# One kernel, several loads reordered: q in one transfer, words behind k and v, the last tile's stores issued by GpSimd

## The chip, the cores and the metric

The kernel runs on one core of a Trainium2 chip. The core has five engines that run their own instruction streams and meet through semaphores: TensorE (PE in the profile; PEld is its loading of weights), VectorE (DVE), ScalarE (ACT), GpSimd (POOL) and SyncE (SP). Here SyncE computes nothing and issues transfers. The transfers of all issuing engines run on the core's 16 DMA engines. The metric is the device time of one execution in microseconds; lower is better. The time before the change is the median of 3 runs, 886.57 us (884.79 to 888.91).

## The reference

```python
def _attn_ref(q, k, v, g_norm):                      # q, k, v: 8 batches, 8 heads, 576 tokens, 64
    kv = np.einsum('bhsd,bhse->bhde', k, v)
    out = np.einsum('bhsd,bhde->bhse', q, kv)
    rms = np.sqrt(np.mean(out * out, axis=-1, keepdims=True) + 1e-06)
    return (out / rms * g_norm).astype(np.float32)

def _moe_ref(x, w_in, w_out):                        # x: 4608 x 512; w_in: 512 x 2048; w_out: 2048 x 512
    h = x @ w_in
    sp = np.where(h > 20.0, h, np.log1p(np.exp(np.minimum(h, 20.0))))
    g = h * np.tanh(sp)
    return (g @ w_out).astype(np.float32)
```

The attention result is laid out as one row of 512 for each of the 4608 tokens and is x of the second function. g_norm is float32 of length 64. The two weight matrices are float64: the kernel sees them as pairs of 32-bit words and joins them to float32 itself.

## The kernel before, in words

Both matrix products of the second function are done by a recursive scheme with 7 block products in place of 8 (Strassen–Winograd). The names A11, S1, S2, A12, S4, S3, A22 are its left operands, and B11, T1 and so on its right ones. To keep fp32 accuracy, each operand is split into a high part (a cast on ScalarE, line 121) and a low part (a subtraction on VectorE, line 122), and each block product is three matmuls per 128 rows.

**Part 1** makes x, and g = mish(x @ w_in), in 9 tiles of 512 tokens. A tile has 4 groups of 7 slots, and so 28 slots in all (`NS`); a group makes g for two of the eight column blocks of each half. A slot is one block product on TensorE (12 matmuls, line 527). `slot(t)` first issues what evicts finished banks (`then`), then the product, then what stands in the plan for that slot (`at`). The order of all engines' work is this order of the program, written out by hand: an instruction waits for everything that stands before it on its engine or queue, and nothing is reordered.

The weights go through `weight_forms` (lines 128 to 178): LOAD (transfers of words by SyncE, line 137), SCALE (ScalarE, line 142), JOIN (three VectorE steps, lines 147 to 149), DIFF (157 to 159), BLOCKS and SUMS (splits, lines 121 and 122). For w_in they are numbered 0 to 7. The words of weights 2 and 5 share the room `wf6`, those of 3 and 6 the room `wf7`, those of 0, 4 and 7 the room `w64`; a load into a room waits until JOIN has read what was there. Weights 0, 1 and 2 are made before slot 0; weights j from 3 to 7 have SCALE and JOIN at slot 3(j−3)+1.

Before slot 0, q of tile 0 comes in four transfers of 128 tokens (`rows_load`, line 295). A partition holds one token of each, and its 64 numbers of a head are one piece of 256 bytes. TensorE turns it with 16 transposes (line 325), the results are copied out (`turned`), and `kv_first_product` (line 234) makes the first batch's product of k and v; `kv_keep` (line 269) copies it out of PSUM, `project` (line 360) multiplies q by it; squares, sums, logarithm and exponential follow (lines 373, 391, 408, 409) and `normalize` (line 430). Tile 1 is loaded and turned in the same way, into one bank pair `x2` for each of its two units, at slots 1 and 8. From tile 2 on (`T32 = 2`) the tiles take another path, which the change leaves alone.

k and v of batch 1 come in four pairs (`k_load`, lines 213 and 214). There are two sets of staging tiles, so the third pair waits for the product of the first (`k_product`, line 252). The last two pairs are issued at slots 1 and 2, their products stand at slots 2 and 3. The loads of weights 6 and 7 stand at slots 1 and 4; in slot 1 the load stands ahead of the third pair of k and v on SyncE's queue.

Each group's results leave by three stores to the DRAM tile `gd` (`put_in`, lines 546, 551, 554), out of the tiles `ula`, `ulb` and `ur`, two buffers each: a buffer is written again two groups later. SyncE issues these stores for tiles 0 to 7, ScalarE those of tile 8.

**Part 2** multiplies g by w_out in 18 groups of 256 tokens. Its preparation runs during tile 8, whose first slot is t8: `g_load(0)` and `g_load(1)` (line 731, 2048 KB each) bring g of the first two groups at slots t8+7 and t8+8. `wo_load` (line 726, 1792 KB each) brings the eight made weights of w_out into the places of w_in's, which come free group by group: two at each of t8+10, t8+17 and t8+24, two at the end. At t8+18, `g_pair` makes the first seven forms for group 0, all in that slot. Group 0 runs as one product over all eight weights (line 863), the others as 7 block products each (line 772). `o_store` (line 793 for tiles 0 and 1, line 804 for the others) writes the output.

Of the kernel before, what the change touches and what calls it, by code (L numbers as in the profile page):

```python
# [27 lines left out]
def linear_attention_rms_mish_ffn(  # L28
# [260 lines left out]
    def rows_load(j, c):  # L289
        for b, s0, cols in segments(j):  # L290
            t0, t1 = max(cols.start, c * P), min(cols.stop, (c + 1) * P)
            if t0 < t1:
                src = q[b, 0:1, s0 + t0 - cols.start:s0 + t0 - cols.start + 1, :]
                src = bass.AP(src.tensor, src.offset, [[D, t1 - t0], [S * D, H], [1, D]])
                nc.sync.dma_start(rows[j][t0 - c * P:t1 - c * P, c, :].rearrange("p (h d) -> p h d", d=D), src)
# [4 lines left out]
    def unit_steps(j, u):  # L300
# [14 lines left out]
        def transpose():  # L315
            if j < T32:
                if j == 0 and u == 1:
                    ps = [bank_new("a").rearrange("p m t -> p (m t)") for _ in range(2)]
                else:
                    x2 = ps_t.tile([P, 2, T], F32, name="x2")  # L320
                    ps = [x2[:, a] for a in range(2)]
                for a in range(2):
                    h = 4 * u + 2 * a
                    for c in range(TR):
                        nc.tensor.transpose(ps[a][:, c * P:(c + 1) * P], rows[j][:, c, h * D:(h + 2) * D], ident)
# [24 lines left out]
        def project():  # L350
# [120 lines left out]
    def at(t, f):  # L471
        plan.setdefault(t, []).append(f)
# [118 lines left out]
    rows[0], turned_q = t[:, 0:2].rearrange("p a (c n) -> p (a c) n", c=TR // 2), t[:, 2].rearrange("p (a t) -> p a t", a=2)  # L591
    for c in range(TR):
        rows_load(0, c)
# [40 lines left out]
    rows[1] = att.tile([P, TR, H * D], F32, name="qs")  # L634
    for c in range(TR):
        rows_load(1, c)
# [7 lines left out]
    weights(2, DIFF)  # L644
    weights(5, LOAD)
# [137 lines left out]
    def o_store(st):  # L783

        i, half = divmod(st["s"], T // G)
        if i < T32:
            for r in range(G // P):
                c = half * G // P + r
                for b, s0, cols in segments(i):
                    t0, t1 = max(cols.start, c * P), min(cols.stop, (c + 1) * P)  # L790
                    if t0 < t1:
                        row = b * S + s0 + t0 - cols.start
                        nc.sync.dma_start(out[row:row + t1 - t0, :], st["o"][t0 - c * P:t1 - c * P, r, :])
            return
# [28 lines left out]
    at(t8 + 8, lambda: g_load(1))  # L823
    at(t8 + 18, lambda: g_pair(gs[0], 0, pair_rooms(0)))
# [128 lines left out]
```

## Time and profile before

| | |
|---|---|
| median of 3 runs | 886.57 us (884.79, 886.57, 888.91) |
| the profiled execution | 885.97 us, span 884.2 us, mean granted clock 0.987 |
| TensorE, matmuls | 828.1 us busy (94%) |
| TensorE, weight loads | 795.7 us (90%) |
| VectorE | 608.7 us (69%) |
| ScalarE | 464.6 us (53%) |
| GpSimd | 4.8 us (1%), 23 instructions, all within the first 6 us |
| DMA | 175.5 MB, mean 199 GB/s |

Times in the rows of the profile are microseconds from the span's start. A row of the timeline gives start, duration, engine, line, operation, what is written and read, and in brackets how long the engine had stood idle before it and what ended that. SPq and ACTq are the queues on which SyncE and ScalarE issue transfers; their rows give issue times, not the time that the data moves. A row of waits gives total, number and longest wait. The chain of waits is followed back from the last instruction and told in order of time. A busy TensorE isn't TensorE at its peak, because matmuls are pipelined.

### The profile page before, as it was taken

The page shows a single profiled execution, that of the slowest core. Times are in us where ns is not written, and L with a number is a line of the kernel's source. Part 1 is how long each engine was busy: PE and PEld are TensorE (multiplying, and loading weights), DVE is VectorE, ACT ScalarE, POOL GpSimd, SP SyncE. Part 2 cuts the span into 40 slices and gives each one's busy share as a digit, 9 for nine tenths or more (in the row PEclk, how much of TensorE's full clock was granted, in tenths as well). Part 3 has the DMA queues.
Part 4 walks back from the last instruction along what each step waited for, and adds up shares of the span by engine and source line. Part 5 has one row for each costly group of instructions (what it writes and reads, how often), then busy time and mean ns, then how long its engine had stood idle before and what let it go on. Part 6 is the DMA issues. An engine that isn't in the chain of part 4 may idle for free.

```text
span 884.2 us, 17156 instructions
## 1 busy us (share of the span) xinstructions
PE 828.1 (94%) x7036; PEld 795.7 (90%) x7036; DVE 608.7 (69%) x804; ACT 464.6 (53%) x703; POOL 4.8 (1%) x23
## 2 busy tenths in 40 slices
PE   4658998998999999999999899999999999999997
PEld 3447898998999999999999789999999999999997
DVE  5869675886777676787764368867777677776772
ACT  3647666556675765666664444344444434434431
POOL 2000000000000000000000000000000000000000
PEclk9969999999999999999999999999999999999999
DMA  9936787987978696767477993344434443334421
GB/s 294 247 114 197 200 274 246 278 263 226 296 219 278 218 304 199 220 204 227 151 227 249 425 416 125 122 150 152 148 121 133 130 120 120 119 120 141 153 65 48
DMA packets 161038, 175.52 MB, mean 199 GB/s; under 512 B 24704, under 2 KB 142464, under 8 KB 159936
## 3 DMA queue, kind: packets, MB, share of 16 engines
q1 hardware_dynamic: 158208, 170.23, 61.8%
q10 hardware_dynamic: 2752, 4.20, 1.3%
q8 instruction: 55, 0.90, 0.4%
q14 instruction: 23, 0.19, 0.1%
HBM read 112.39 MB, written 62.00 MB: 197 GB/s over the span
## 4 chain that ended last, share of the span: by engine, by line
PE 63%; DMA 11%; DVE 10%; ACT 9%; issue 4%; SPq 2%; ACTq 0%; DVEq 0%
PE a L772 22%; PE bc L772 16%; PE a L527 13%; PE bc L527 7%; DMA gd<-ula 5%; PE s L252 2%; DMA vm<-in_v_dram 2%; DVE ur L548 1%; DMA wod<-wst 1%; ACT L412 1%; ACT gf L121 1%; DMA rd<-fl 1%; DVE gf L122 1%; DVE fa L122 1%; ACT L118 1%
## 5 line engine op out<-in xcount | busy, mean ns | idle before, releaser
L772 PE MATMUL a<-wf,gf 128*128 128x256 f32 x1632 | 201.8, 283 | 0.5 <-DVE ur L812 0.5
L772 PEld LDWEIGHTS a<-wf,gf 128*128 128x128 f32 x1632 | 198.4, 192 | 0.7 <-DVE ur L812 0.7
L122 DVE TENSOR_TENSOR gf<-g,gf 128x1024 fp32r<-128x1024 f32 (+1 forms) x123 | 132.9, 1087 | 90.7 <-ACT gf L121 90.7
L527 PE MATMUL a<-gf,wf 128*128 128x256 f32 x1296 | 173.0, 287 | 11.5 <-DVE gf L430 4.5
L527 PEld LDWEIGHTS a<-gf,wf 128*128 128x128 f32 x1296 | 162.9, 193 | 18.1 <-ACT ur L504 6.6
L527 PE MATMUL bc<-gf,wf 128*128 128x256 f32 x1296 | 170.3, 285 | 3.5 <-ACT ur L495 2.4
L527 PEld LDWEIGHTS bc<-gf,wf 128*128 128x128 f32 x1296 | 161.4, 191 | 5.1 <-ACT ur L495 2.6
L121 ACT CAST gf<-g 128x1024 fp32r<-128x1024 f32 (+1 forms) x123 | 114.6, 939 | 93.3 <-DVE g L752 65.1
L772 PE MATMUL bc<-wf,gf 128*128 128x256 f32 x1224 | 152.7, 283 | 1.0 <-DVE gf L122 1.0
L772 PEld LDWEIGHTS bc<-wf,gf 128*128 128x128 f32 x1224 | 149.4, 192 | 1.4 <-ACT gf L121 0.7
L527 PE MATMUL a<-a,wf 128*128 128x256 f32 x432 | 59.8, 289 | 2.5 <-DVE ur L548 2.5
L527 PEld LDWEIGHTS a<-a,wf 128*128 128x128 f32 x432 | 55.8, 195 | 5.6 <-DVE ur L548 3.1
L118 ACT ACTIVATE ur<-ur 128x1024 f32<-128x1024 f32 x36 | 38.1, 1059 | 37.1 <-DVE ur L548 37.1
L122 DVE TENSOR_TENSOR fa<-fl,fh 128x1024 fp32r<-128x1024 f32 x28 | 34.3, 1224 | 22.1 <-ACT fh L121 21.2
L504 ACT COPY ur<-a 128x512 f32<-128x512 f32 (+1 forms) x53 | 27.3, 516 | 37.6 <-PE a L772 24.6
L122 DVE TENSOR_TENSOR gf<-gf 128x512 fp32r<-128x512 f32 x45 | 30.4, 689 | 24.0 <-ACT gf L121 24.0
L121 ACT CAST gf<-a 128x1024 fp32r<-128x1024 f32 x17 | 17.9, 1052 | 53.5 <-DVE a L749 50.9
L121 ACT CAST gf<-gf 128x512 fp32r<-128x512 f32 x45 | 27.1, 618 | 31.4 <-DVE gf L451 19.1
L495 ACT COPY ur<-bc 128x512 f32<-128x512 f32 (+1 forms) x53 | 27.4, 517 | 29.9 <-PE bc L772 23.0
L548 DVE TENSOR_TENSOR ula<-bc,ula 128x512 f32<-128x512 f32 x36 | 24.8, 688 | 25.4 <-PE bc L527 25.3
L118 ACT ACTIVATE ula<-ula 128x512 f32<-128x512 f32 x36 | 22.8, 633 | 22.1 <-DVE ula L548 22.1
L252 PE MATMUL s<-vm,km 128*64 128x64 f32 x448 | 20.1, 235 | 14.1 <-DMA vm<-in_v_dram 14.1
(137 smaller groups left out, 858.1 us busy)
## 6 DMA issues: line engine op xcount, KB each, us to landing
g<-gd SPq DMA_DIRECT2D x18, 2048.0 KB, 8.9
gd<-ur SPq DMA_DIRECT2D x32, 512.0 KB, 4.0
wod<-wst SPq DMA_DIRECT2D x16, 896.0 KB, 5.6
wf<-wod SPq DMA_DIRECT2D x8, 1792.0 KB, 16.2
gd<-ula SPq DMA_DIRECT2D x32, 256.0 KB, 5.1
gd<-ulb SPq DMA_DIRECT2D x32, 256.0 KB, 4.3
w<-in_moe_w_out_dram SPq DMA_DIRECT2D x32, 256.0 KB, 4.6
km<-in_k_dram SPq DMA_DIRECT2D x28, 256.0 KB, 4.8
```

Source lines behind the costliest of these rows:

```text
L118: nc.scalar.activation(o, i, AF.Mish)
L121: nc.scalar.copy(hi, src)
L122: nc.vector.tensor_sub(lo, src, hi.bitcast(F32))
L252: nc.tensor.matmul(kvps[o * D:(o + 1) * D, b % 2, h0 // 2 + i, :], kt, vt, start=(c == 0), stop=(c == CM))
L412: nc.scalar.preload_act_table_set("natural_log_exp_and_others")
L495: then(t + 2, lambda: nc.scalar.copy(dst(st, "22"), st["c"]))
L504: then(t + 4, lambda: nc.scalar.copy(dst(st, "12"), st["a"]))
L527: nc.tensor.matmul(bank[:, jj], w[:, right, a, kc, :], xf[:, b, kc, :], start=first and jj == kc == s == 0, stop=(kc == 1 and s == 2), ski ...
L548: nc.vector.tensor_add(o, bank, o)
L772: nc.tensor.matmul(bank, gf[:, a, c, :], wo[c][:, right, b, :], start=first and c == s == 0, stop=(c == NF2 - 1 and s == 2), skip_group_ch ...
```

## The change

- q of tiles 0 and 1 comes in one transfer for each segment (one for tile 0, two for tile 1). A partition now holds four neighbouring tokens, so that a piece is 1024 bytes. Columns of these two tiles therefore stand in another order; `project` picks a segment's columns out by a view, and `o_store` writes rows back in their order, two rows in one piece.
- A turn of 128 columns by a transpose becomes two matmuls against the identity, one for each head, with 64 columns of q as the stationary operand and the identity as the moving one.
- The copies `turned` of unit 1 go ahead of the SUMS of weights 0; SCALE and JOIN of weights 1 go behind the first `kv_keep`.
- The loads of g_norm are issued by GpSimd instead of SyncE, ahead of its other work.
- The load of weights 4 moves from before slot 0's preparation to its end, ahead of that of weights 5. The loads of weights 6 and 7 move from slots 1 and 4 to slots 3 and 6.
- The stores of tile 8 are issued by GpSimd instead of ScalarE.
- `g_load(1)` moves from slot t8+8 to t8+26; the first forms of part 2's group 0 are made one per slot, at t8+17 to t8+23.

```diff
+    def spots(cols):
+
+        return slice(cols.start // TR, cols.stop // TR)
+
+    def rows_load(j):
         for b, s0, cols in segments(j):
-            t0, t1 = max(cols.start, c * P), min(cols.stop, (c + 1) * P)
-            if t0 < t1:
-                src = q[b, 0:1, s0 + t0 - cols.start:s0 + t0 - cols.start + 1, :]
-                src = bass.AP(src.tensor, src.offset, [[D, t1 - t0], [S * D, H], [1, D]])
-                nc.sync.dma_start(rows[j][t0 - c * P:t1 - c * P, c, :].rearrange("p (h d) -> p h d", d=D), src)
+            p = spots(cols)
+            src = q[b, 0:1, s0:s0 + 1, :]
+            src = bass.AP(src.tensor, src.offset, [[TR * D, p.stop - p.start], [S * D, H], [1, TR * D]])
+            nc.sync.dma_start(rows[j][p], src)
...
-                    h = 4 * u + 2 * a
                     for c in range(TR):
-                        nc.tensor.transpose(ps[a][:, c * P:(c + 1) * P], rows[j][:, c, h * D:(h + 2) * D], ident)
+                        for o in range(2):
+                            src = rows[j][:, 4 * u + 2 * a + o, c * D:(c + 1) * D]
+                            nc.tensor.matmul(ps[a][o * D:(o + 1) * D, c * P:(c + 1) * P], src, ident, start=True, stop=True)
...
-                        nc.tensor.matmul(ps[:, c], kvf[b][:, hp, :], st["q"][:, a, c], start=True, stop=True)
+                        o, r = (t.rearrange("p (c n) -> p c n", n=P)[:, :, spots(c)] for t in (ps, st["q"][:, a]))
+                        nc.tensor.matmul(o, kvf[b][:, hp, :], r, start=True, stop=True)
...
-        eng = nc.sync if i < NT - 1 else nc.scalar
+        eng = nc.sync if i < NT - 1 else nc.gpsimd
...
-    for c in range(TR):
-        rows_load(0, c)
+    rows_load(0)
...
-        nc.sync.dma_start(gcol[r, :], g_norm.rearrange("(p o) -> p o", o=1))
+        nc.gpsimd.dma_start(gcol[r, :], g_norm.rearrange("(p o) -> p o", o=1))
     weights(2, LOAD)
-    weights(4, LOAD)
     weights(3, LOAD)
...
     do(0, 0, "turned")
+    do(0, 1, "turned")
     weights(0, SUMS)
-    do(0, 1, "turned")
-    weights(1, SCALE, JOIN)
     kv_first_product(first)
     kv_keep(0, first)
+    weights(1, SCALE, JOIN)
     do(0, 0, "project", "square")
...
     weights(2, DIFF)
+    weights(4, LOAD)
     weights(5, LOAD)
...
-            at(t, lambda j=j: weights((6, 7)[j - 3], LOAD))
+            at(t + 2, lambda j=j: weights((6, 7)[j - 3], LOAD))
...
+            for b, s0, cols in segments(i):
+                p = spots(cols)
+                row = b * S + s0 + half * G // P
+                dst = out[row:row + 1, :]
+                dst = bass.AP(dst.tensor, dst.offset, [[TR * DM, p.stop - p.start], [DM, G // P], [1, DM]])
+                nc.sync.dma_start(dst, st["o"][p])
...
-    at(t8 + 8, lambda: g_load(1))
-    at(t8 + 18, lambda: g_pair(gs[0], 0, pair_rooms(0)))
+    at(t8 + 26, lambda: g_load(1))
+    first_rooms = []
+    for n, f in enumerate(MADE):
+        def first_form(f=f):
+            if f == MADE[0]:
+                first_rooms.extend(pair_rooms(0))
+            gs[0]["f"][f, 0] = g_form(gs[0], f, slice(0, 2), first_rooms[f // 4][:, f % 4])
+        at(t8 + 17 + n, first_form)
```

More of the change, by code (lines that the diff above doesn't have):

```diff
@@ L287, in segments @@
         return segs
-    def rows_load(j, c):
+    def spots(cols):
+        return slice(cols.start // TR, cols.stop // TR)
+    def rows_load(j):
         for b, s0, cols in segments(j):
-            t0, t1 = max(cols.start, c * P), min(cols.stop, (c + 1) * P)
-            if t0 < t1:
-                src = q[b, 0:1, s0 + t0 - cols.start:s0 + t0 - cols.start + 1, :]
-                src = bass.AP(src.tensor, src.offset, [[D, t1 - t0], [S * D, H], [1, D]])
-                nc.sync.dma_start(rows[j][t0 - c * P:t1 - c * P, c, :].rearrange("p (h d) -> p h d", d=D), src)
+            p = spots(cols)
+            src = q[b, 0:1, s0:s0 + 1, :]
+            src = bass.AP(src.tensor, src.offset, [[TR * D, p.stop - p.start], [S * D, H], [1, TR * D]])
+            nc.sync.dma_start(rows[j][p], src)
     rows = {}
@@ L590, in linear_attention_rms_mish_ffn @@
     t = wfp.tile([P, 3, 2 * T], F32, name="wf2")
-    rows[0], turned_q = t[:, 0:2].rearrange("p a (c n) -> p (a c) n", c=TR // 2), t[:, 2].rearrange("p (a t) -> p a t", a=2)
-    for c in range(TR):
-        rows_load(0, c)
+    rows[0], turned_q = t[:, 0:2].rearrange("p a (h n) -> p (a h) n", h=H // 2), t[:, 2].rearrange("p (a t) -> p a t", a=2)
+    rows_load(0)
     kv0 += [wfp.tile([P, NKC, 9 * D], F32, name=f"wf{n}") for n in (3, 4)]
@@ L633, in linear_attention_rms_mish_ffn @@
     k_load(1, 1)
-    rows[1] = att.tile([P, TR, H * D], F32, name="qs")
-    for c in range(TR):
-        rows_load(1, c)
+    rows[1] = att.tile([P, H, TR * D], F32, name="qs")
+    rows_load(1)
     do(0, 1, "square", "sums")
@@ L786, in o_store @@
         if i < T32:
[L787 to L793, printed above, removed]
+            for b, s0, cols in segments(i):
[4 more added lines that the diff above has]
+                nc.sync.dma_start(dst, st["o"][p])
             return
```

## The prediction

> **What bounds the kernel now.** First view: TensorE's waits over the whole span (us in total, times, longest); the row on top:
>
> ```profile
> PE s L252 <- DMA vm<-in_v_dram: 14.1, 3, 12.9
> ```
>
> TensorE is otherwise nearly always busy, so its gaps are what an edit of order can win. Of the 14.1 us that it waits for v, 12.9 are one wait, for batch 1. The second view, the timeline around it:
>
> ```profile
> 35.19 12.57 SPq L137 DMA_DIRECT2D wf<-in_moe_w_in_dram  x4
> ...
> 45.55 1.23 DVE L149 SCALAR_TENSOR_TENSOR fl<-wf,fl 128x1024 uint32<-128x1024 uint32 x1
> ...
> 47.86 0.45 SPq L213 DMA_DIRECT2D km<-in_k_dram  x1
> ...
> 51.73 1.22 DVE L122 TENSOR_TENSOR wf<-wd,wf 128x1024 fp32r<-128x1024 f32 x1
> ...
> 54.62 1.12 PE L252 MATMUL s<-vm,km 128*64 128x64 f32 x16 [12.88 <-DMA vm<-in_v_dram]
> ...
> 59.05 0.58 ACT L504 COPY ur<-a 128x512 f32<-128x512 f32 x1 [7.70 <-PE a L527]
> ...
> 60.69 0.69 DVE L147 TENSOR_SCALAR fl<-fl 128x1024 uint32<-128x1024 uint32 x1 [7.74 <-ACT fl L142]
> ...
> 71.75 1.22 PE L325 MATMUL x<-ident,qs 128*128 128x128 f32 x8 [2.54 <-ACT gf L378]
> ```
>
> SyncE holds four word transfers from 35.19 on: weights 5 and weights 6. Weights 6 go into the room that weights 3 are read from, and the last reader is the join at L149, done at 46.78. The k and v loads of slots 1 and 2 stand behind them in SyncE's order, so they leave at 47.86 and v is used at 54.62. But VectorE had work of its own until 52.95 (the L122 at 51.73), and idled only 7.7 us before 60.69. That is the part of the 12.9 us that nothing else covers.
>
> Third, the last tile, where the loads for part 2 run:
>
> ```profile
> 472.34 2.29 SPq L731 DMA_DIRECT2D g<-gd  x2
> ...
> 478.31 34.25 SPq L726 DMA_DIRECT2D wf<-wod  x8
> ...
> 497.39 1.69 PE L527 MATMUL bc<-gf,wf 128*128 128x256 f32 x12 [1.11 <-DVE ula L548]
> ...
> 501.11 1.70 PE L527 MATMUL a<-gf,wf 128*128 128x256 f32 x12 [0.59 <-ACT ula L490]
> ...
> 505.96 0.58 ACT L495 COPY ur<-bc 128x512 f32<-128x512 f32 x1 [4.91 <-DMA gd<-ur]
> ...
> 506.60 1.70 PE L527 MATMUL bc<-gf,wf 128*128 128x256 f32 x12 [2.36 <-ACT ur L495]
> ...
> 510.52 1.70 PE L527 MATMUL a<-a,wf 128*128 128x256 f32 x12 [0.78 <-DVE ur L548]
> ...
> 524.57 0.41 ACT L121 CAST gf<-g 128x256 fp32r<-128x256 f32 x1 [2.94 <-issue]
> ...
> 534.03 3.04 PE L772 MATMUL a<-wf,gf 128*128 128x256 f32 x24
> ...
> 480.00:532.00 52.00, 45.84 (x372) 44.62 (x371) 24.05 (x55) 21.21 (x45) 0.00 (x0) 1.00 1.01 407
> ```
>
> The last row is a view by stretches (PE, PEld, DVE, ACT, POOL busy, clock, DMA share, GB/s): the DMA engines are full. A store of the last tile takes 14 to 23 us, its buffer comes free late, and ScalarE, which also issues these stores, stands still.
>
> **The change part by part.** The profiled execution took 885.97 us (span 884.2 and 1.8 around it), 0.6 below the median of 886.57; I sum against it.
>
> *k and v ahead of the words.* Weights 6 and 7 move two slots back. The two k and v pairs then leave when their staging buffers come free, after the products at 36.47 and 39.77, about 38 and 41. Ahead of them in the queues lie weights 4 (moved here) and 5, 2.1 MB, some 6 us at the 350 to 380 GB/s that the start shows. In the chain of waits v lands 5.4 us after its issue:
>
> ```profile
> 49.06 5.43 DMA vm<-in_v_dram
> ```
>
> There it had the words of weights 6 ahead of it; with another 3 us for what is left of weights 4 and 5, it lands near 44 to 48. VectorE needs the next product (L527, slot 3) out of the way by about 51, so VectorE's order decides: gain **7.7 us**. Bounds: 12.9 if VectorE's order gave way too, 4 if the loads land near 51. Next late is ScalarE's L378 before L325, as now. Weights 4, 6 and 7 are wanted at slots 4, 10 and 13, over 10 us after they can land.
>
> *First q by one transfer.* Each descriptor grows from 256 B to 1 KB. The rates by 1.5 us slices of the first 60 us:
>
> ```profile
> GB/s 0 126 384 320 220 218 239 378 384 358 358 389 361 325 363 348 352 351 346 317 289 185 183 231 218 280 359 93 0 0 5 12 232 382 331 284 238 7 0 0
> ...
> 10.99 1.33 PE L325 MATMUL x<-ident,wf 128*128 128x128 f32 x5 [0.60 <-DMA wf<-in_q_dram]
> ...
> 12.11 1.91 PE L325 MATMUL a<-ident,wf 128*128 128x128 f32 x8
> ...
> 14.35 2.39 PE L234 MATMUL s<-wf,wf 64*64 64x64 f32 x72 [0.32 <-DMA wf<-in_v_dram]
> ...
> 36.47 1.12 PE L252 MATMUL s<-vm,km 128*64 128x64 f32 x16
> ...
> 39.77 0.69 PE L252 MATMUL s<-vm,km 128*64 128x64 f32 x16
> ...
> 40.65 1.09 PE L325 MATMUL x<-ident,qs 128*128 128x128 f32 x8
> ```
>
> q ran at about 220 GB/s, beside 384 before and after. The words and q are 2.1 MB: reached near 9.8 us now, and at 384 from 3 us on near 8.0. The last rows were used 1.2 us behind, so all of q is there at 9.2 instead of 11.0. But the first quarter was used at 7.59; now nothing turns before 9.2. v, and with it the first k·v product, could start near 12.5 instead of 14.35.
>
> *The turns by matmul.* One transpose (16 for a tile) becomes two fp32 matmuls of 64 columns against the identity, and each fp32 matmul is two instructions here (36 at L234 show as 72). So 32 instructions replace 8 for each of the two units. The trace has none of this shape. Nearest: L252, with the same 128*64 weights but 64 moving columns, 43 ns each (0.69/16), 70 ns after a pause. With 128 moving columns I take twice that: 86 and 140 ns. Below stands half of a present turn (two column halves side by side): 0.136/2 = 68 ns, early 0.239/2 = 120. Above: a whole one, 136 and 239. The early price lasts 3.4 us here (10.99 to about 14.4). From 9.2, 64 instructions then take 3.4 us for the first 24 and 40·0.086 = 3.4: done at 16.0, against 14.02 now; bounds 15.0 and 19.4. So TensorE's turns, not v, hold the first product: **+2.0** (+1.0 to +5.4).
>
> *Words of weights 1 after the first kv_keep.* The order on ScalarE now:
>
> ```profile
> 17.32 1.12 ACT L142 ACTIVATE fl<-wf 128x1024 f32<-128x1024 f32 x1 [3.01 <-DMA wf<-in_moe_w_in_dram]
> ...
> 18.34 0.51 ACT L269 COPY kvf<-s 64x128 f32<-64x128 f32 x2
> ...
> 23.75 1.05 ACT L121 CAST wf<-wd 128x1024 fp32r<-128x1024 f32 x1
> ...
> 24.82 1.27 ACT L408 ACTIVATE fa<-bc,eps 128x512 f32<-128x512 f32 x2
> ```
>
> The product ends at 16.74, yet L269 waits for the scale to 18.34. Counted from the end of the turns (14.02), the logarithms of L408 start at +10.8. New order: product to +2.7, keep to +3.25, scale to +4.4, join 3.2 (to +7.6), differences 1.55 (L157 to L159, +9.2), cast 1.05, L408 at +10.25. Gain **0.55**, so the start is 1.45 later in sum (+0.45 to +4.85). From there VectorE has hardly a gap to 52.95, and the delay carries through.
>
> *Second turns of tile 1.* Those of unit 0 stand at 40.65, before the v wait, and cost nothing while v lands after about 43 (1.7 us if that cover is gone). Those of unit 1 are the 1.22 us at 71.75, behind which the chain of waits runs on TensorE alone: 32·0.086 = 2.75, **+1.5** (+0.95 to +3.1).
>
> *Last tile.* Moving the second g (2.1 MB, 5.1 us at 0.41 MB/us) behind six of the eight word loads takes it out of the line that the stores of the second group stand in. That stores share that line is read from their landing (the first row of the ula stores, the second such row of weights 6 and 7 of w_out; queue 10 is ScalarE's, with packets and MB):
>
> ```profile
> DMA to landing us min/median/max: 6.8/14.9/23.0
> ...
> 489.12 0.34 ACTq L554 DMA_DIRECT2D gd<-ur  x1
> ...
> 478.31 5.87 SPq L726 DMA_DIRECT2D wf<-wod  x1
> ...
> q10 hardware_dynamic: 2752, 4.20, 1.3%
> ...
> 486.30 14.09 DMA gd<-ula
> ...
> L726 SPq DMA_DIRECT2D wf<-wod x2: 319/320/320, 511.5 to 512.2; - x2
> ...
> DMA to landing us min/median/max: 12.3/14.6/16.9
> ...
> 543.30 3.10 PE L772 MATMUL bc<-wf,gf 128*128 128x256 f32 x24 [0.48 <-DVE gf L122]
> ...
> 546.96 3.11 PE L772 MATMUL bc<-wf,gf 128*128 128x256 f32 x24 [0.56 <-DVE gf L122]
> ```
>
> The store at 476.2 landed in 6.8 us, when the 4.2 MB of both g, begun at 474, were through (484). That of 486.30 took 14.09; less 5.1 it lands at 495, before its buffer is wanted at 500.47, and the one of 489.12 (16.8 us) at 501, before 505. Forms one per slot take the 1.11 at 497.39, where L548 stood behind a burst of seven forms. Issued by GpSimd, a store's wait for an earlier one (2.94 us at 524.57) holds no other engine: GpSimd has nothing else to do there. Together 1.11+0.59+2.36+0.78 = 4.84 before 512. But the bytes to be loaded stay the same and the DMA engines are full to the end, so the last word load lands where it did, 512.2+16.9 = 529.1. The 21 products that use it take 2.5: part 2's next group starts at 531.6, not 534.03. Gain 2.4, and the 0.48 and 0.56 that VectorE's late start left: **3.4 us**. Above: 5.9 (4.84 and 1.04) if the loads end earlier. Below: GpSimd issues no transfer in this trace; nearest are 0.34 us for one on ScalarE and 5.87 for the longest on SyncE, so a landing some 5 us later is possible, which brings the old stalls back (gain 1), and 10 us later costs about 5.
>
> The Trainium skill (SBUF — State Buffer, "two separate sides") speaks against this part: GpSimd writes the descriptors itself and is locked out of its port while VectorE runs in a two-port mode; its advice is to issue from ScalarE or SyncE. No run here shows a GpSimd transfer; by that page the gain of this part would shrink towards the lower bounds above, 880 to 886.
>
> Two transfers fewer for tile 1's q, stores of the first two tiles in larger pieces, and g_norm's by GpSimd lie behind TensorE work or at free queues: 0; without that cover a few tenths each.
>
> Sum: −7.7+2.0−0.55+1.5−3.4 = −8.15; 885.97−8.15 = 877.8, and 0.6 to the median: **878 us**.
>
> **Rivals.**
> *The turns cost a full one each*: +4.85 and +3.1 in place of 1.45 and 1.5: 883. For it: nothing shows two column halves running at once at this width; against: L252's 43 ns is below the half of 0.136.
> *The last tile gives nothing*, since the GpSimd stores land as late as ScalarE's did: 882; up to 886 with a loss of 5. For it: full DMA engines; against: the 5.1 us of g are gone from the line.
> *More than forecast*: turns at the low bound and the last tile at 5 or more: 874.
> *Slower*: GpSimd takes so long to make its descriptors that every store lands 15 us later. Place: the copies into ula and ur in the last tile's third group; price: about 10 us there, 886.6−8.15+3.4+10 = 892. It decides above 10 us of delay. For it: VectorE is busy 24 of 52 us there; against: a group's stores are only 43 packets on each DMA engine (2752 over 4 groups and 16 engines).
> *The change doesn't remove the stall*, because weights 4 and 5 hold the queue and v lands after 51: −4 in place of −7.7: 882.
>
> **How the numbers follow.** Forecast (876 to 881) 0.50, turns dear 0.13, last tile nothing 0.17, more 0.10, stall stays in part 0.06, slower 0.04. Changes under 0.5% (4.4 us) can't be told from none. Faster by that is below 882.1: the forecast, the better case, half of the 882 and 883 cases: 0.78; same 0.18; slower 0.04. The range 872 to 884 leaves out the end of the worse last-tile cases and the slower one.
>
> **What would show it.** The wait of L252 for v before 55 falls to a few us and VectorE has no 7.7 us gap; L325's 32 instructions take near 3.4 us each unit early and 2.75 later; L234 starts near 16; ScalarE's waits for gd stores in the last tile are gone and L772 starts about 2.4 us earlier relative to the tile's start. It is wrong if the first product starts after 18, if gd stores by GpSimd land later than 15 us, or if VectorE still idles before weights 4.

## The result, and the profile after

The changed kernel takes **881.34 us** (median of 7 runs, 879.63 to 883.15), the kernel before 886.2 in the same comparison: a ratio of 0.9935, 95% interval 0.9911 to 0.9958. It is faster by 0.65%. 878 was forecast; the time lies within the range on record. But the terms of the sum didn't all hold: two errors at the start nearly cancel in the profile below, and the last tile's gain is missing.

The profiled execution took 879.63 us (span 877.8), against 885.97 (span 884.2). It is the fastest of the seven, 1.71 below their median. In the tables below a product's start is read from TensorE's timeline. "Mark" is the same group of 24 bc products in tile 8 of every kernel, at 480.28 before and 473.93 after (some expectations on record call it the last one of the second-last tile; it is tile 8's own). "Predicted" is the shift by the prediction's own terms.

| place | before | after | shift | predicted |
|---|---|---|---|---|
| first block product | 34.23 | 35.32 | +1.09 | +1.45 |
| second turns of tile 1 | 71.75 | 65.11 | −6.64 | −6.25 |
| the sums behind them (ss) | 75.46 | 70.09 | −5.37 | −4.75 |
| mark | 480.28 | 473.93 | −6.35 | −4.75 |
| first block product of part 2 | 534.03 | 529.12 | −4.91 | −7.15 |
| end of the span | 884.2 | 877.8 | −6.4 | −8.15 |

TensorE's waits over the whole span of the kernel after (total, times, longest):

```profile
PE q L871 <- DMA wf<-wod: 6.0, 1, 6.0
...
PE s L252 <- DMA vm<-in_v_dram: 1.2, 2, 0.9
```

The 14.1 us for v are 1.2. New are 6.0 us for words of w_out, in the last tile. The timeline of the kernel after around the place of the old wait:

```profile
42.51 0.37 SPq L213 DMA_DIRECT2D km<-in_k_dram  x1
...
47.35 0.69 PE L252 MATMUL s<-vm,km 128*64 128x64 f32 x16 [0.37 <-DMA vm<-in_v_dram]
...
52.86 1.22 DVE L122 TENSOR_TENSOR wf<-wd,wf 128x1024 fp32r<-128x1024 f32 x1
54.05 0.69 DVE L147 TENSOR_SCALAR fl<-fl 128x1024 uint32<-128x1024 uint32 x1
54.69 3.55 PE L365 MATMUL x<-fh,kvf 128*128 128x448 f32 x6 [2.12 <-ACT kvf L269]
...
65.11 3.42 PE L329 MATMUL x<-ident,qs 128*64 128x128 f32 x32 [2.56 <-ACT gf L383]
```

VectorE goes from its split at 52.86 straight into the next join; its gap of 7.74 us is gone. The second turns start 6.64 us earlier: 7.74 less the 1.09 that the start lost. What is late next is ScalarE's L383, as forecast (L378 before).

The start of the kernel after, by its timeline:

```profile
10.87 3.24 PE L329 MATMUL x<-ident,wf 128*64 128x128 f32 x32 [10.87 <-DMA wf<-in_q_dram]
13.93 1.93 PE L329 MATMUL a<-ident,wf 128*64 128x128 f32 x32
15.79 2.31 PE L234 MATMUL s<-wf,wf 64*64 64x64 f32 x72
...
18.20 0.53 ACT L269 COPY kvf<-s 64x128 f32<-64x128 f32 x2 [2.10 <-PE s L234]
```

q is there at 10.87 and not at 9.2. The turns take 101 ns an instruction at first (3.24/32) and then 60 (1.93/32), each below the low bound of the prediction (120 and 68). They end at 15.8, where 16.0 was forecast, and the first product of k and v begins as they end.

This start differs from run to run. The six kernels of the next section that are the same program up to slot 0 (words ahead of k and v, stores by ScalarE, second g early, last tile as before, later bytes, still later bytes) have their turns begin between 10.78 and 11.87 and take 5.5 to 6.2 us instead of 5.0, and their first block product starts at 35.78 to 37.30. In all seven it comes 19.52 to 19.54 us behind the first product of k and v; in the kernel before it came 19.89 behind.

The last tile, by TensorE's timeline and the issues of SyncE and GpSimd:

```profile
473.93 3.04 PE L532 MATMUL bc<-gf,wf 128*128 128x256 f32 x24
...
499.35 1.70 PE L532 MATMUL a<-a,wf 128*128 128x256 f32 x12 [0.78 <-DVE ur L553]
500.89 5.20 PE L871 MATMUL q<-wf,g 128*128 128x256 f32 x42
505.93 10.24 PE L871 MATMUL q<-wf,gf 128*128 128x256 f32 x84
522.21 7.07 PE L871 MATMUL q<-wf,gf 128*128 128x256 f32 x42 [6.04 <-DMA wf<-wod]
529.12 3.04 PE L775 MATMUL a<-wf,gf 128*128 128x256 f32 x24
...
505.32 0.57 POOL L559 DMA_DIRECT2D gd<-ur  x1 [7.09 <-ACT ur L118]
...
500.36 11.41 SPq L729 DMA_DIRECT2D wf<-wod  x2
516.16 0.52 SPq L734 DMA_DIRECT2D g<-gd  x1
```

Of the four old waits, which summed to 4.84 us, only the 0.78 is left. But the 42 products that use the last two words wait 6.04 us for the first of these two, and then take 7.07 us instead of the 5.20 that the first 42 products take. The landing of the last words and the clock, by the groups of tile wf and by stretches (PE, PEld, DVE, ACT, POOL busy, clock, DMA share, GB/s):

```profile
L729 SPq DMA_DIRECT2D wf<-wod x4: 319/480/10680, 492.1 to 511.1; - x4
...
DMA to landing us min/median/max: 15.3/15.3/15.3
...
520.00:525.00 5.00, 2.79 (x13) 2.82 (x14) 4.83 (x5) 1.07 (x2) 0.00 (x0) 0.50 0.98 403
```

The last word leaves at 511.1 and lands 15.3 later, at 526.4: 52.5 us behind the mark. In the kernel before it was 512.2 + 16.9 = 529.1, 48.8 behind its mark. The second-last one, at which the wait ends, is there at 522.2, 48.3 behind the mark; before, it was 511.5 + 12.3 = 523.8, 43.5 behind. So the two land 3.7 and some 4.7 us later in the course of the tile, though SyncE turns to them 4.8 us earlier (26.4 us behind the mark instead of 31.25) and is then held 10.68 us in the first of the two issues.

What moved from the issue of g(0) to the landing of the last word, by queue (packets, MB): first the kernel before (472.34 to 529.16), then the one after (466.00 to 526.46). q1 is SyncE's queue:

```profile
q1 hardware_dynamic: 5552, 19.14, 84.5%
q10 hardware_dynamic: 2342, 3.59, 16.7%
...
q1 hardware_dynamic: 6262, 19.86, 83.9%
q0 software_dynamic: 1216, 4.20, 17.1%
```

Issued by GpSimd, the tile's stores of ula land like this (the row answers to 6.8/14.9/23.0 before; below it GpSimd's queue over the whole span, answering to q10's 2752 packets for the same 4.20 MB):

```profile
L556 POOL DMA_DIRECT2D gd<-ula x4: 727/736/749, 468.4 to 497.5; - x4
...
DMA to landing us min/median/max: 6.5/9.3/12.6
...
q0 software_dynamic: 1280, 4.20, 1.2%
```

### The profile page after: what moved, and what is told of

It is laid out like the page before. It is cut to its first block, busy times and chain, and to the rows that moved or that the text cites. A ratio compares the mean times of both kernels' runs of the same rounds, so it can differ in the third digit from the quotient of the medians.

```text
span 877.8 us, 17344 instructions
## 1 busy us (share of the span) xinstructions
PE 831.5 (95%) x7132; PEld 800.7 (91%) x7132; DVE 608.8 (69%) x804; ACT 465.3 (53%) x703; POOL 14.1 (2%) x37
## 3 DMA queue, kind: packets, MB, share of 16 engines
q0 software_dynamic: 1280, 4.20, 1.2%
## 4 chain that ended last, share of the span: by engine, by line
PE 72%; DMA 8%; ACT 7%; DVE 6%; issue 4%; SPq 2%; DVEq 0%; ACTq 0%
PE a L775 22%; PE bc L775 17%; PE a L532 16%; PE bc L532 9%; PE s L252 3%; DMA wf<-wod 2%; PE q L871 1%; DMA wf<-in_moe_w_in_dram 1%; DVE ur L553 1%; ACT L417 1%; DMA vr<-in_v_dram 1%; DMA rd<-fl 1%; SPq L137 1%; DVE fa L122 1%; ACT L118 1%
## 5 line engine op out<-in xcount | busy, mean ns | idle before, releaser
L553 DVE TENSOR_TENSOR ula<-bc,ula 128x512 f32<-128x512 f32 x36 | 24.7, 687 | 23.3 <-PE bc L532 23.1
L118 ACT ACTIVATE ula<-ula 128x512 f32<-128x512 f32 x36 | 22.8, 633 | 22.8 <-DVE ula L553 22.8
L553 DVE TENSOR_TENSOR ur<-bc,ur 128x512 f32<-128x512 f32 x36 | 24.4, 677 | 7.7 <-ACT ur L509 4.3
```

The lines of the kernel that those rows point to most:

```text
L118: nc.scalar.activation(o, i, AF.Mish)
L553: nc.vector.tensor_add(o, bank, o)
```

## The experiments

All are edits of the changed kernel. "Stretch" is the time from the mark to the first block product of part 2, "rest" the time from there to the end of the span; both come from the profile, the time and ratio from the runs beside the kernel before. Its median was between 885.5 and 887.2 us in the five comparisons, so kernels of different comparisons are set side by side by their ratios.

| kernel | median us | ratio, 95% interval | stretch | rest |
|---|---|---|---|---|
| before | | 1 | 53.75 | 350.2 |
| after | 881.34 | 0.9935 (0.9911–0.9958) | 55.19 | 348.7 |
| words ahead of k and v | 888.29 | 1.0013 (1.0002–1.0023) | 55.33 | 348.8 |
| stores by ScalarE | 883.95 | 0.9956 (0.9935–0.9977) | 58.51 | 349.7 |
| second g early | 881.57 | 0.9937 (0.9920–0.9953) | 55.26 | 348.7 |
| last tile as before | 881.56 | 0.9955 (0.9940–0.9970) | 53.91 | 350.2 |
| old q | 880.08 | 0.9918 (0.9901–0.9936) | 55.74 | 348.7 |
| q ahead of weights 0 | 880.48 | 0.9940 (0.9921–0.9958) | 55.20 | 348.7 |
| later bytes | 878.70 | 0.9925 (0.9909–0.9941) | 53.62 | 348.5 |
| old q, later bytes | 879.50 | 0.9927 (0.9911–0.9944) | 53.75 | 348.9 |
| q first and turned first, later bytes | 880.09 | 0.9933 (0.9918–0.9947) | 52.95 | 348.5 |
| still later bytes | 876.88 | 0.9883 (0.9863–0.9903) | 50.45 | 348.8 |

**Words ahead of k and v** puts the loads of weights 6 and 7 back and leaves those of weights 4 where the change has them.

```diff
-            at(t + 2, lambda j=j: weights((6, 7)[j - 3], LOAD))
+            at(t, lambda j=j: weights((6, 7)[j - 3], LOAD))
```

> Only the loads of weights 6 and 7 go back to slots 1 and 4, ahead of the third pair of k and v. Theory (VectorE's order had covered all of the wait but 7.7 us): TensorE waits for v of batch 1 until about 55 again, VectorE idles 7 to 8 us before the join of weights 4, and the kernel is 7 to 8 us slower than the changed one, 888 to 890. Rival (later stages had slack that took part of the gain): 3 to 5 us slower, 885 to 886.

The ratio rises by 0.0078, 6.9 us of 886 (4.6 to 9.2 by the two intervals, an estimate). Its timeline has the old wait back, and VectorE's gap:

```profile
56.07 1.12 PE L252 MATMUL s<-vm,km 128*64 128x64 f32 x16 [11.50 <-DMA vm<-in_v_dram]
...
61.95 0.69 DVE L147 TENSOR_SCALAR fl<-fl 128x1024 uint32<-128x1024 uint32 x1 [6.99 <-ACT fl L142]
```

The wait is 11.50, the gap 6.99, the price 6.9. The second turns of tile 1 come 36.77 us behind the first block product here, 29.79 in the changed kernel: 6.98 later. It is the gap of VectorE, not the wait of TensorE, that gives the size.

**Stores by ScalarE** and **second g early** each undo one part of the last tile.

```diff
-        eng = nc.sync if i < NT - 1 else nc.gpsimd
+        eng = nc.sync if i < NT - 1 else nc.scalar
```

> Only the stores of the last tile go back from GpSimd to ScalarE. Theory (the loads bind: the end of the last two word loads is set by the bytes that are moved before it, and by GpSimd's stores 1.6 MB more come before it): ScalarE waits for stores again, but the first block product of part 2's second group starts no later, or up to 3.5 us earlier, counted from the tile; time 878 to 881.5. Rival (the stores' waits bind): TensorE's waits of 2 to 4 us in the last tile come back in full, time 883 to 885.

```diff
-    at(t8 + 26, lambda: g_load(1))
+    at(t8 + 8, lambda: g_load(1))
```

> Only the load of g for part 2's second group goes back from slot t8+26 to t8+8. Theory (the loads bind): stores in the last tile land some 5 us later, TensorE waits 1 to 4 us for their buffers, and the wait for the last word loads (6 us) shrinks by as much; time within 1 us of the changed kernel, 880.5 to 882.5. Rival (the stores' waits bind): 3 to 4 us slower, 884 to 885.

With the stores by ScalarE, its own copy into ula waits for the store of that buffer, which left at 480.88 and, by the profile's wait, was through at about 501.7, 20.8 us later:

```profile
480.88 0.37 ACTq L556 DMA_DIRECT2D gd<-ula  x1
...
501.68 0.58 ACT L495 COPY ula<-a 128x512 f32<-128x512 f32 x1 [9.63 <-DMA gd<-ula]
...
502.32 2.93 PE L532 MATMUL a<-gf,wf 128*128 128x256 f32 x12 [8.53 <-ACT ula L495]
```

The second g is late in this kernel, and yet this store takes 20.8 us where it took 14.09 before. Issued by GpSimd in the changed kernel, it takes 8.7. The late g does not bring the stores forward. The stretch is 3.3 us longer than the changed kernel's, and the expectation of 878 to 881.5 missed; 883.95 is what its rival had. The times alone don't settle it, since the ratio is only 0.0021 above the changed kernel's and the intervals overlap.

With g early and the stores by GpSimd, no copy waits for a store, where 1 to 4 us of such waits were expected. The words bind all the same (TensorE's waits in the last tile):

```profile
PE q L871 <- DMA wf<-wod: 4.5, 3, 2.7
PE q L871 <- DVE gf L122: 1.4, 1, 1.4
```

SyncE is not held at the last two words here (0.32 us each), and the last one lands 52.6 us behind the mark all the same: the hold of 10.68 us is not what made it late. So it is the issue by GpSimd that took the old waits away, and the place of the second g moves nothing in sum.

**Last tile as before** undoes the three edits of that tile together.

```diff
-        eng = nc.sync if i < NT - 1 else nc.gpsimd
+        eng = nc.sync if i < NT - 1 else nc.scalar
...
-    at(t8 + 26, lambda: g_load(1))
-    first_rooms = []
-    for n, f in enumerate(MADE):
...
-        at(t8 + 17 + n, first_form)
+    at(t8 + 8, lambda: g_load(1))
+    at(t8 + 18, lambda: g_pair(gs[0], 0, pair_rooms(0)))
```

> The changed kernel with all of its last tile as the kernel before has it: ScalarE issues the four sets of stores of tile 8, g(1) is loaded at slot t8+8 and the forms of the first pair are made in one slot; k, v, q and the order of the start stay as changed. Theory (the loads of part 2's words set the end of tile 8, and each byte that is moved ahead of them costs): the stretch from the last bc group of the second-last tile to the first part-2 product takes the 53.7 us that it took in the kernel before, against 55.2 changed, so the time is 1 to 2 us under the changed kernel, 879 to 880.5 us, and the TensorE waits for ScalarE's evictions (about 4 to 5 us) are back. Rival (the changed last tile is worth the 3.4 us that the prediction gave it, and something else in the changed profile took it back): 55 us or more in that stretch, and 883 to 885 us.

The old waits are back, with their old lengths:

```profile
493.05 1.70 PE L532 MATMUL bc<-gf,wf 128*128 128x256 f32 x12 [1.12 <-DVE ula L553]
...
502.27 1.70 PE L532 MATMUL bc<-gf,wf 128*128 128x256 f32 x12 [2.36 <-ACT ur L500]
...
539.11 3.10 PE L775 MATMUL bc<-wf,gf 128*128 128x256 f32 x24 [0.47 <-DVE gf L122]
```

The stretch is 53.91, 1.28 shorter than the changed one, as the theory had it; but the rest is 350.2 again, 1.5 longer, as the last row shows it begin. Both edges count, and by the profiles the sum is level: from the mark to the end of the span are 404.1 us here, 403.9 in the changed kernel and 403.9 in the kernel before. The time missed the expected 879 to 880.5 for that reason. By the profiles, then, the changed last tile as a whole is worth nothing. The ratio is 0.0020 above the changed kernel's (1.8 us), but the intervals overlap and can't tell that from nothing.

**Later bytes** keeps GpSimd's stores for three groups, issues those of the fourth by SyncE behind the words, and loads g(2) later.

```diff
-        eng = nc.sync if i < NT - 1 else nc.gpsimd
+        eng = nc.sync if i < NT - 1 or n == NQ - 1 else nc.gpsimd
...
-    g_load(2)
     ahead(AHEAD)
+    g_load(2, nc.scalar)
```

> The changed kernel with fewer bytes ahead of the last words: the stores of the last of tile 8's four groups are issued by SyncE, behind the loads of weights 6 and 7 in its queue, and g(2) is loaded by ScalarE behind the first three forms of part 2. Theory (the words bind, bytes ahead of them cost): the wait of TensorE for the words (6.0 us) falls by 2 to 4 us, the stretch from the last bc group of the second-last tile to the first part-2 product takes 51.5 to 53.5 us against 55.2, and the time is 877.5 to 880 us. Rival (what holds the last words is the queue of their own engine and not the bytes beside them): the wait stays at 5 to 6 us and the time at 881 to 882; or g(2), coming later, gives TensorE a new wait of 1 us or more for g in the first products of part 2.

```profile
520.58 7.89 PE L871 MATMUL q<-wf,gf 128*128 128x256 f32 x42 [3.65 <-DMA wf<-wod]
...
520.00:525.00 5.00, 4.42 (x21) 4.45 (x22) 3.81 (x4) 1.93 (x2) 0.00 (x0) 0.50 0.98 394
```

The wait falls from 6.04 to 3.65, the stretch to 53.62 (a little above the expected 51.5 to 53.5), the time to 878.7. By its ratio that is 0.9 us under the changed kernel, which the intervals can't tell from nothing; the stretch shows the effect. The loads did set the end, and bytes beside them cost. What is left of the price is now nearly as much clock as wait: 42 products take 7.89 us in place of 5.20.

**Still later bytes** moves the third group's stores behind the words too.

```diff
-        eng = nc.sync if i < NT - 1 else nc.gpsimd
+        eng = nc.sync if i < NT - 1 or n >= NQ - 2 else nc.gpsimd
+        late = 8 if i == NT - 1 and n == NQ - 2 else 0
...
-            at(t + 2, lambda: eng.dma_start(left[:, :, TH:T], o))
+            at(t + 2 + late, lambda: eng.dma_start(left[:, :, TH:T], o))
```

(and the same `late` in the two other stores, with the later g(2))

> As the run with the later bytes of the last tile, and the third group's stores of tile 8 (another 1.05 MB, 2.5 us at 0.42 MB/us) also go by SyncE behind weights 6 and 7. Theory (bytes ahead of the words cost, and a TensorE that waits long loses clock behind it): the wait for the words falls from 3.65 to about 1 us, the 42 products behind it take 5.2 to 6 us instead of 7.9, and the stretch from the last bc group of the second-last tile to the first part-2 product takes 50 to 51.5 us against 53.6: 875.5 to 877.5 us in all. Rival (the stores' buffers are the next bound: part 2 writes its first output into the tile that the third group's last store still reads): ScalarE's copy of part 2's first results waits 2 us or more, and the time is 878 to 881.

```profile
519.87 2.75 PE L872 MATMUL q<-wf,gf 128*128 128x256 f32 x21 [1.40 <-DMA wf<-wod]
524.07 2.78 PE L872 MATMUL q<-wf,gf 128*128 128x256 f32 x21 [1.45 <-DMA wf<-wod]
526.68 3.04 PE L776 MATMUL a<-wf,gf 128*128 128x256 f32 x24
...
520.00:525.00 5.00, 3.55 (x28) 3.34 (x29) 4.80 (x5) 1.11 (x2) 0.00 (x0) 1.00 0.99 394
```

Stretch 50.45, time **876.88 us**, both as the theory had them; ScalarE's copy into ur waits 0.7 us, so that rival falls. The wait itself fell only from 3.65 to 2.85, in two pieces, where about 1 was expected; most of the 3.2 us of the stretch came from the clock, which stays at 1.00 here: the 42 products take 5.53 us (2.75 + 2.78) in place of 7.89. This version beats both kernels: its interval ends (0.9903) below where that of the changed one begins (0.9911).

**Old q** (with its layout, its `project` and its output rows, of which only the loads and turns are shown), and two tries to start the turns earlier.

```diff
-    rows_load(0)
+    for c in range(TR):
+        rows_load(0, c)
...
-                        for o in range(2):
-                            src = rows[j][:, 4 * u + 2 * a + o, c * D:(c + 1) * D]
-                            nc.tensor.matmul(ps[a][o * D:(o + 1) * D, c * P:(c + 1) * P], src, ident, start=True, stop=True)
+                        nc.tensor.transpose(ps[a][:, c * P:(c + 1) * P], rows[j][:, c, h * D:(h + 2) * D], ident)
```

> Tiles 0 and 1 as before the change (q in pieces of 256 bytes, four and five transfers, transposes of 128 columns, output rows in their old places); all the rest as changed. Theory (one transfer of q gains nothing, since q moved at some 230 GB/s with 1 KB pieces too, and its turns by matmul cost more): the first block product starts at 33.5 to 34.5 in place of 35.3 and the second turns take 1.3 us less; 2 to 3 us faster than the changed kernel, 878.5 to 879.5. Rival (k and v issued 4 us earlier make the first q's change a gain): 1 to 2 us slower, 882.5 to 883.5.

```profile
14.23 2.31 PE L234 MATMUL s<-wf,wf 64*64 64x64 f32 x72
...
33.76 2.50 PE L527 MATMUL a<-gf,wf 128*128 128x256 f32 x10 [4.55 <-DVE gf L430]
...
63.52 1.97 PE L325 MATMUL x<-ident,qs 128*128 128x128 f32 x8 [4.11 <-ACT gf L378]
```

Four transfers and sixteen transposes start the block products 1.56 us earlier than the new q does, and up to 3.5 earlier than the other kernels with the new q. Again the first block product comes 19.5 us behind the first product of k and v. Yet the mark stands at 475.65, 1.7 us later. From the first product of tile 1 (at 107.57 here) to the mark this kernel takes 368.1 us, while the nine kernels with the new q take 364.6 to 365.2. By its ratio the time is 1.5 us under the changed kernel's, which the intervals can't tell from nothing. The same layout with the later bytes takes 366.7 there, and its time is no better than that of the later bytes alone:

> The changed kernel with the first and second q in the layout and transfers of the kernel before (four transfers of 256-byte pieces, sixteen transposes each), and with the later bytes of the last tile (last group's stores by SyncE behind weights 6 and 7, g(2) by ScalarE behind the first forms). Theory (the two steps lie in different stages and add: the old q starts the first block product 1.5 us earlier and its second turns cost 1.3 us less, the later bytes gain 2.6 us): first block product at 33.5 to 34 us, last tile 53 to 54 us, 876.5 to 878.5 us in all. Rival (what q gains early is lost again before tile 8, as the profile with the old q alone shows 3.3 us lost between 105 and 475 us): 878 to 880 us.

It measured 879.5, so the rival holds: what q gains early is given back before tile 8. Where exactly wasn't settled; small waits of TensorE for v (2.5 us against 0.9 in the changed kernel) and for ScalarE's copies are longer in it, in several places.

```diff
-    weights(0, LOAD)
     t = wfp.tile([P, 3, 2 * T], F32, name="wf2")
...
     rows_load(0)
+    weights(0, LOAD)
```

> The changed kernel with the transfer of q issued ahead of that of weights 0. Theory (q's transfer moves at about 230 GB/s whatever is beside it, so it lands about 1.05 MB / 230 GB/s = 4.6 us after its first byte, and its place in the queue sets when): q lands at 6.5 to 8.5 us against 10.87, the first block product starts 2 to 3.5 us earlier (32 to 33.5 against 35.3), unless weights 0, about 3.5 us later, hold ScalarE's first scaling; the gain that is left at 105 us is 0 to 2 us, and the time 879 to 881.5 us. Rival (q's rate at the start is that of all transfers then, so that the order changes nothing but who is first): q lands at 9 us or later and weights 0 later than 11, and the time is that of the changed kernel or up to 2 us over it, 881 to 884 us.

```profile
6.60 3.68 PE L329 MATMUL x<-ident,wf 128*64 128x128 f32 x32 [6.60 <-POOL sel L612]
...
13.82 2.31 PE L234 MATMUL s<-wf,wf 64*64 64x64 f32 x72 [1.56 <-DMA wf<-in_v_dram]
...
16.04 1.00 ACT L342 COPY fh<-x 128x1024 f32<-128x1024 f32 x1
...
35.39 1.01 PE L532 MATMUL a<-gf,wf 128*128 128x256 f32 x3 [4.56 <-DVE gf L435]
```

q lands before 6.6 (the row names a fill by GpSimd as what the turns waited for last), 4.3 us earlier, and the first block product doesn't move: 35.39 against 35.32. It comes 21.6 us behind the first product of k and v, not 19.5: weights 0 come 3.3 us later, and ScalarE's copy of the turned q stands behind their cast. The last try keeps q first and moves the copies ahead of weights 0, with the later bytes:

```diff
-    weights(0, SCALE, JOIN, DIFF)
     do(0, 0, "transpose")
     do(0, 1, "transpose")
-    weights(0, BLOCKS)
     do(0, 0, "turned")
     do(0, 1, "turned")
-    weights(0, SUMS)
+    weights(0, SCALE, JOIN, DIFF)
+    weights(0, BLOCKS, SUMS)
```

> The changed kernel with q's transfer ahead of that of weights 0, both copies of the turned q ahead of weights 0 in ScalarE's and VectorE's order, and the later bytes of the last tile. Theory (with q first, it was the copy of the turned q, queued behind weights 0's cast on ScalarE, and the v that lands at 13.8 that held the first projection): turns at 6.6, first k-v product still at about 13.8, first projection at 16.8 to 17.5 (18.5 with q first alone), first block product 33.5 to 34.5 against 35.4, total 876.5 to 878.5. Rival (weights 0, 3.4 us late, hold VectorE, whose split work is the bound of the first 50 us): first block product unchanged at 35 or later, total 878 to 880.

```profile
10.60 1.01 ACT L342 COPY fh<-x 128x1024 f32<-128x1024 f32 x1 [8.57 <-PE x L329]
...
13.42 2.31 PE L234 MATMUL s<-wf,wf 64*64 64x64 f32 x72 [0.76 <-DMA wf<-in_v_dram]
...
37.48 2.93 PE L532 MATMUL a<-gf,wf 128*128 128x256 f32 x12 [4.55 <-DVE gf L435]
```

The copy comes 5.4 us earlier and the first block product 2.1 later, 24.1 us behind the first product of k and v. The rival holds for these two kernels: once q is first, weights 0 and what VectorE and ScalarE do to them set the start. In the changed kernel itself it is still the turns of q: its program with the latest q (last tile as before) has q 1.0 us later, turns 1.0 longer and its first block product 2.0 later.

## Why the prediction was right, and where it was wrong

- **k and v ahead of the words, −7.7:** right in mechanism and size. The bound was VectorE's own work up to 52.95 and not the 12.9 us of the wait; 7.73 measured between the two profiles (−6.64 − 1.09), 6.98 between the changed kernel and the one with the edit undone.
- **q at 9.2:** wrong. It lands at 10.87, 0.1 us earlier than its last piece before. The step that failed is "at 384 from 3 us on". The rates by 1.5 us slices of the first 60 us of the kernel after:

```profile
GB/s 0 126 377 241 219 372 392 390 360 351 378 387 365 350 350 349 328 282 207 155 219 251 240 300 350 348 290 204 187 196 189 19 39 331 366 318 44 0 13 251
```

  Pieces of 1 KB still show 241 and 219 between 4.5 and 7.5 us, where q begins, so that the 2.1 MB of the words and q are reached near 9.2 and not 8.0. And 2.7 MB have moved by 10.87: the sum put at nothing the bytes of k and v, which are issued at 2.35 and 3.60 here (7.13 and 8.32 before) and move beside q. With q ahead of weights 0 it lands before 6.6, so the piece size alone isn't the limit; what makes the dip between the two transfers stays open.
- **The turns, done at 16.0, +2.0:** right by two errors that nearly cancel. In this profile they start 1.7 us late, take 5.0 us instead of 6.8 and delay the first product of k and v by 1.44; in the six other profiles they take 5.5 to 6.2 and delay it by 1.9 to 3.4. That TensorE's turns, and not v, hold this product came true. Early, an instruction takes 101 ns here and 115 in the six others; later, at 42.7 us, 62. So halving a present turn (120 and 68) did not bound them from below, and the rival of dear turns (883) is out.
- **kv_keep, −0.55:** right in mechanism, −0.36 in size (19.53 from the first product of k and v to the first block product, against 19.89).
- **The sum of the start, +1.45:** +1.09 in this profile, +1.5 to +3.1 in the six others. That the profile agrees with the sum is luck in part.
- **Second turns, +1.5:** from their start to the sums it is 4.98 against 3.71, +1.27, but not for the forecast reason alone. The 32 instructions take 3.42 us in place of 2.75: the granted clock is 0.50 up to 68.1, behind a wait of 2.56 us. And with the old transposes in the changed order (old q) the same stretch takes 4.46. So the turn by matmul accounts for some 0.5 us of it in this profile.
- **Between there and the mark** the prediction had nothing, and about 1.0 us was gained. From the first product of tile 1 to the mark the kernel before takes 365.4 us, the nine kernels with the new q 364.6 to 365.2, the two with the old q 368.1 and 366.7. The layout of q or what comes with it is likely to play a part; no run splits it further.
- **Last tile, −3.4:** wrong, and the main reason why 878 became 881. Of the 4.84 us, 4.06 went as forecast. The step that failed is "the bytes to be loaded stay the same ..., so the last word load lands where it did". The bytes ahead of it did not stay the same: the fourth group's stores of ur and ulb (0.79 MB) leave 31 us behind the mark instead of 43, and g(2) (2.1 MB) is issued at 516.16 in place of 530.29, both before the last word lands. By the queues' rows, 0.6 MB more of stores and 0.7 MB more of SyncE's loads had moved when it landed; at 0.40 MB/us that is 3.3 us (an estimate), and it landed 3.7 us later. TensorE waits 6.04 us, and the 42 products behind the wait take 1.87 us more. In all, +1.44 in the stretch in place of −2.4; the rest gains 1.5 (1.04 forecast). Level, as the kernel with the old last tile shows. The two runs with later bytes confirm the cause: each step that takes bytes out of the way shortens the stretch (55.19, 53.62, 50.45), and the bytes that move up to the last word's landing fall from 24.1 to 23.1 and 22.1 MB (22.8 before).
- **From 878 to 881:** 3.35 us by the last tile, less 1.6 that came back before the mark. Another 1.1 is that the profiled run lies 1.71 below its median, where the forecast added 0.6 for this; the rest is rounding.
- **The second g out of the stores' line:** refuted. With ScalarE's issue and the late g the second group's store takes 20.8 us, and while it was under way 7.45 MB moved on SyncE's queue and 1.37 on ScalarE's. The stores land early because GpSimd issues them: with g early, those of ula take 8.7 us by GpSimd (median, second g early) and 14.7 by ScalarE (last tile as before). The trace before had a sign that there is no common line: the second g landed 17.5 us after its issue, at 490.5 and not at 484 as the prediction read it, and the store of 476.2, issued behind it, at 483.0.
- **Rivals:** "the last tile gives nothing" came true in size (882), for another reason than its own: GpSimd's stores land earlier, not as late. The slower rival is out: an issue takes GpSimd 0.57 to 0.75 us.

On that last point the Trainium skill (SBUF — State Buffer, "two separate sides") had spoken against GpSimd. VectorE was busy 31.8 of the 52 us from 480 on, and no issue of a store took over 0.75 us and no store of ula over 12.6: the trace does not show the lock-out here. Whether VectorE ran in a two-port mode at all in these 52 us the trace does not tell. The part's gain was lost, but by the words.

## What to carry to other kernels

When the DMA engines are full, the landing of the load that binds goes by the bytes that move before it: freeing a stall lets later stores and loads start earlier, and they then move before the transfer that binds next. List what will move ahead of the last needed load, and push behind it whatever is wanted later. Don't count on the order of issue between the queues of different engines: here a store by ScalarE landed later when there was less ahead of it. The size of a removed wait is read from the engine that sets the pace behind it (7.7 us of VectorE's gap, not the 12.9 us of TensorE's wait). And a shift between two profiles is read from an event that both share: here the start moved by 2 us between profiles of one and the same program, while the stretches behind it agreed to some tenths.

## What the runs showed of the hardware

- **A wait of TensorE costs twice.** After waits of 6.04 and 3.65 us the granted clock of the next stretch was 0.50, and 42 products took 7.07 and 7.89 us instead of 5.20; after two waits of 1.4 us it stayed at 1.00. The Trainium skill (TensorE: Matmul & The Clock Gate, "What's actually happening") gives a window of about 3.4 us of idleness after which the clock is halved. By that rule the long waits come out right, but here shorter ones were enough too: behind the waits of 2.12 us (up to 54.69) and 2.56 us (up to 65.11) the clock was 0.50 as well (clock, DMA share and GB/s stand last):

```profile
54.50:57.80 3.30, 3.11 (x7) 1.88 (x7) 3.22 (x5) 1.99 (x6) 0.00 (x0) 0.50 0.00 0
64.80:68.10 3.30, 2.99 (x28) 2.99 (x30) 3.20 (x4) 2.48 (x5) 0.00 (x0) 0.50 0.03 5
```

  In the last variant, going from one wait of 3.65 us to two of 1.4 saved 0.8 us of waiting and 2.4 us in the 42 products behind it. Whether splitting a wait of the same length saves as much wasn't tried.
- **The issuer changes how a store travels.** The same 4.20 MB of stores went in 2752 packets from ScalarE and 1280 on GpSimd's queue (g_norm's 64 included). With nothing but the issuer changed, the second group's store of ula took 20.8 us by ScalarE and 8.7 by GpSimd. The Trainium skill (DMA: Bandwidth & Descriptors, "Issuing engines are not separate DMA queues") says that issuing from several engines saves only issue time; here the measurement differs. Whether the packets or the queue make the difference wasn't tried.
- **An issue can block its engine.** One load's issue held SyncE for 10.68 us (0.32 for the quickest). What stands behind it in program order waits as long: the last word's load was issued only at 511.1.
- **fp32 matmuls on half the columns** (128 moving columns, 64 stationary) run at 62 ns an instruction at 42.7 us (1.97 us for 32), where a full-width transpose of the same length took 136 at 40.65 before (1.09 us for 8). Four of the instructions replace one transpose, so a turn costs about 0.25 us in place of 0.14.
